# Gathering heads by DMA in every group instead of selector matmuls, in a two-layer transformer kernel

## The chip, the cores and the metric

The kernel runs on one core of a Trainium2 chip. The metric is the device time of one execution in microseconds (us). Engines are named as in the profile: PE is TensorE, PEld its weight loads, DVE is VectorE, ACT is ScalarE, POOL is GpSimd, and SP issues most DMAs.

## The reference, cut to what matters

```python
x = A_x                                              # 1 x 2048 x 1024, bfloat16
for layer in range(2):                               # written out twice in the reference
    q, k, v = split_heads(layernorm(x) @ wqkv)       # 32 heads of 32
    # each position attends to itself and 7 earlier ones, 2 apart
    idx    = pos[:, None] - 2 * arange(8)[None, :]
    logits = einsum("bhsd,bhswd->bhsw", q, k[idx]) * 32 ** -0.5   # -1e9 where idx < 0
    attn   = softmax(logits)
    x = x + merge(einsum("bhsw,bhswd->bhsd", attn, v[idx])) @ wo
    x = x + gelu(layernorm(x) @ w1 + b1) @ w2 + b2   # 3584 wide
```

## The kernel before

The work is done in eight groups (two layers times four blocks of 512 tokens). For a group `n`, PE computes QKV(n), WO(n), FFN1(n) and FFN2(n), one after the other without a gap. The attention itself is on DVE and is hidden under PE's matmuls of other groups. These are its parts (`P` is 128, `H` 32 heads, `NTT` 4 token tiles, `HP` 4, `W` 8 taps):

```python
def new_prod(n, c):            # q * k for the 8 taps of one chunk c, summed over chunks as a tree
    prod = bigp.tile([P, NTT, W, P], BF16, name="big")      # the pool "big" has 3 buffers
    vec.tensor_tensor(out=prod[:], in0=q..., in1=win_by_tile(k...), op=ALU.mult)
    ...                        # additions into the tree's open tiles

def head_sum(n, last=True):    # groups 0 and 1: the partitions of a head summed by selector matmuls
    for wh in range(2):
        for tb in range(NTT):
            mm(L[tb * H:(tb + 1) * H, wh * 4:(wh + 1) * 4, :], lhsT=smat[:], rhs=prod[:, tb, ...], ...)

def gather(n):                 # groups 2 to 7: moved by DMA, added on DVE
    Lq = bigp.tile([P, HP, W, P], BF16, name="big")
    for tb in range(NTT):
        pool.dma_start(Lq[tb * H:(tb + 1) * H, :, :, :], prod[:, tb, :, :])

def attend(n):                 # softmax over the 8 taps
    ...                        # e = the sum over a head, from Lq or from head_sum
    vec.tensor_reduce(out=mx[:], in_=L[:].rearrange("p w t -> p t w"), axis=AX.X, op=ALU.max)
    vec.tensor_tensor(out=e[:], in0=L[:], in1=mx..., op=ALU.subtract)
    act.activation(e[:], e[:], ACT.Exp, scale=SCALE)
    vec.tensor_reduce(out=z[:], in_=e[:].rearrange("p w t -> p t w"), axis=AX.X, op=ALU.add)
    vec.reciprocal(z[:], z[:])
    vec.tensor_tensor(out=a[:], in0=e[:], in1=z..., op=ALU.mult)

def spread(n):                 # the weights of a head to all its partitions, through DRAM
    for tb in range(NTT):
        pool.dma_start(a_d[:, :, tb * P:(tb + 1) * P], a[tb * H:(tb + 1) * H, :, :])
    for j in range(HP):
        pool.dma_start(abc[j::HP, :, :], a_d[:, :, :])

def av(n, c):                  # weights * v for one chunk: one product, three additions
    pv = bigp.tile([P, W, T], BF16, name="big")
    vec.tensor_tensor(out=pv[:], in0=s["abc"][:], in1=win(s["vT"][:, c, :]), op=ALU.mult)
    ...
    vec.tensor_tensor(out=s["oT"][:, c, :], in0=pv[:, 0, :], in1=pv[:, 1, :], op=ALU.add)
```

WO(n) contracts over the eight chunks of `oT`, so its first tile needs all eight. The order in which the parts are recorded, cut to the start:

```python
stage(q1, sides=at(6, attend, 0) + at(6, spread, 0) + at(6, hold) + each(new_prod, 1, 8, 1, 0, 4) + each(av, 0, 12, 1))
stage(q2, 18)                        # the first 18 of the 24 chunks of QKV(2)
new_prod(1, 4)
hold()
stage(gen_wo(0))
...
stage(gen_ffn1(0), sides=at(5, attend, 1) + at(5, spread, 1) + at(5, hold) + each(new_prod, 2, 2, 1)
      + at(10, gather, 2) + at(10, hold) + each(av, 1, 10, 2, 0, 4))
for n in range(1, N - 2):
    ...
    if n + 3 < N:
        stage(gen_ffn2(n), sides=at(0, attend, n + 2) + at(2, ln_a, n + 3))
```

`hold` makes every later DVE instruction stay behind what was recorded so far. Between holds a scheduler orders DVE's instructions.

## Time and profile before

| | before |
|---|---|
| time, median of 3 runs | 1232.97 us (1232.96 to 1233.32) |
| profiled span | 1231.1 us |
| PE busy | 1226.2 us, 5,789 matmuls |
| chain of waits | PE 99% |

The page's busy table of the kernel before:

```profile
PE 1226.2 (100%) x5789; PEld 632.7 (51%) x5789; DVE 870.0 (71%) x892; ACT 307.1 (25%) x491; POOL 123.0 (10%) x230
```

PE works all the time. Only fewer matmul columns, or a wait that goes away, could make the kernel faster, and there are hardly any waits. DVE is idle for 29% of the span on average, but an average says little about the stage where it is late. The timeline of PE shows where WO(0) and WO(1) stand. Its columns are start, duration, engine, source line, operation, output from input, shapes, count, and in brackets the idle time before with what ended it:

```profile
119.79 5.78 PE L118 MATMUL acc<-xnT,wt 128*128 128x512 bf16 x26
125.40 13.99 PE L118 MATMUL acc<-wt,oT 128*128 128x512 bf16 x64
139.23 20.88 PE L118 MATMUL acc<-xnT,wt 128*128 128x512 bf16 x96
...
246.94 13.98 PE L118 MATMUL acc<-wt,oT 128*128 128x512 bf16 x64
...
398.88 13.98 PE L118 MATMUL acc<-wt,oT 128*128 128x512 bf16 x64
```

The lines with `oT` are WO(0), WO(1) and WO(2). None has a wait in front, and each takes 13.98 to 13.99 us. The timeline of DVE tells how close that is. AV(0) begins and ends with these lines:

```profile
89.88 4.49 DVE L93 TENSOR_TENSOR big<-abc,vT 128x4096 bf16<-128x4096 bf16 x2
94.29 3.56 DVE L93 TENSOR_TENSOR big<-big 128x2048 bf16<-128x2048 bf16 x4
97.76 0.76 DVE L93 TENSOR_TENSOR oT<-big 128x512 bf16<-128x512 bf16 x2
98.43 4.49 DVE L93 TENSOR_TENSOR big<-abc,vT 128x4096 bf16<-128x4096 bf16 x2
...
123.41 0.76 DVE L93 TENSOR_TENSOR oT<-big 128x512 bf16<-128x512 bf16 x2
```

The eight chunks run in pairs (`x2`, `x4`): 8.55 us for two. The last `oT` is written at 124.2 us, 1.2 us before WO(0) starts.

### The profile page before, as it was taken

The page shows a single profiled execution, that of the slowest core. Times are in us where ns is not written, and L with a number is a line of the kernel's source. Part 1 is how long each engine was busy: PE and PEld are TensorE (multiplying, and loading weights), DVE is VectorE, ACT ScalarE, POOL GpSimd, SP SyncE. Part 2 cuts the span into 40 slices and gives each one's busy share as a digit, 9 for nine tenths or more (in the row PEclk, how much of TensorE's full clock was granted, in tenths as well). Part 3 has the DMA queues.
Part 4 walks back from the last instruction along what each step waited for, and adds up shares of the span by engine and source line. Part 5 has one row for each costly group of instructions (what it writes and reads, how often), then busy time and mean ns, then how long its engine had stood idle before and what let it go on. Part 6 is the DMA issues. An engine that isn't in the chain of part 4 may idle for free.

```text
span 1231.1 us, 13996 instructions
## 1 busy us (share of the span) xinstructions
PE 1226.2 (100%) x5789; PEld 632.7 (51%) x5789; DVE 870.0 (71%) x892; ACT 307.1 (25%) x491; POOL 123.0 (10%) x230
## 2 busy tenths in 40 slices
PE   9999999999999999999999999999999999999999
PEld 7666544456444564445544465444654444444444
DVE  8989899995996999376992779927599698012001
ACT  4343152014310143202431024310244101400310
POOL 3010011101021102200031000210000102000000
PEclk9999999999999999999999999999999999999999
DMA  9954677756487658756476565766666569546441
GB/s 301 289 179 142 177 220 183 210 140 230 147 197 226 177 165 180 220 170 186 149 187 222 172 171 169 174 222 196 171 183 157 186 200 198 166 158 196 153 136 53
DMA packets 219359, 226.63 MB, mean 184 GB/s; under 512 B 68562, under 2 KB 187488, under 8 KB 216224
## 3 DMA queue, kind: packets, MB, share of 16 engines
q1 hardware_dynamic: 214704, 208.69, 57.1%
q0 software_dynamic: 4592, 17.05, 5.7%
q8 instruction: 45, 0.74, 0.2%
q14 instruction: 18, 0.15, 0.0%
HBM read 197.40 MB, written 6.29 MB: 165 GB/s over the span
## 4 chain that ended last, share of the span: by engine, by line
PE 99%; DVE 0%; DMA 0%; ACT 0%; issue 0%
PE acc L118 99%; DMA x<-in_A_x_dram 0%; DVE stats L93 0%; PE acc L213 0%; PE L L118 0%; PE L L213 0%; ACT xnT L93 0%; DVE xn L93 0%; DVE x L93 0%; DVE mv L93 0%; PE acc L183 0%; DVE rstd L93 0%
## 5 line engine op out<-in xcount | busy, mean ns | idle before, releaser
L118 PE MATMUL acc<-xnT,wt 128*128 128x512 bf16 (+1 forms) x3392 | 720.8, 375 | 0.0
L118 PEld LDWEIGHTS <-wt 128*128 128x128 bf16 x3392 | 400.3, 119 | 318.8 <-issue 1.6
L118 PE MATMUL acc<-wt,hT 128*128 128x512 bf16 (+1 forms) x1820 | 388.1, 376 | 0.0
L118 PEld LDWEIGHTS <-hT 128*128 128x128 bf16 x1820 | 178.1, 98 | 209.0
L93 DVE TENSOR_TENSOR big<-big 128x2048 bf16<-128x2048 bf16 (+2 forms) x184 | 245.6, 1360 | 2.9
L93 ACT ACTIVATE hT<-acc,b1T 128x512 bf16<-128x512 f32 x224 | 152.5, 688 | 331.3 <-PE acc L118 331.2
L93 DVE TENSOR_TENSOR big<-qT,kT 128x4096 bf16<-128x4096 bf16 x64 | 143.8, 2286 | 26.7 <-ACT kT L93 26.1
L93 DVE TENSOR_TENSOR big<-abc,vT 128x4096 bf16<-128x4096 bf16 x64 | 144.8, 2287 | 24.3 <-DMA abc<-a_d 23.7
L93 DVE TENSOR_TENSOR tmp<-acc,b2bc 128x512 f32<-128x512 f32 x56 | 38.7, 690 | 148.4 <-PE acc L118 144.9
L93 ACT CAST qT<-acc 128x512 bf16<-128x512 f32 (+1 forms) x72 | 38.0, 542 | 341.4 <-PE acc L118 341.4
L118 PE MATMUL acc<-wt,oT 128*128 128x512 bf16 x448 | 97.9, 379 | 0.0
L93 DVE BATCH_NORM_STATS2 stats<-x 128x6 f32<-128x512 bf16 x128 | 83.5, 680 | 3.3 <-DMA x<-in_A_x_dram 2.6
L118 PEld LDWEIGHTS <-oT 128*128 128x128 bf16 x448 | 43.9, 98 | 52.8
L93 DVE TENSOR_TENSOR x<-acc,big 128x512 bf16<-128x512 f32 (+1 forms) x9 | 5.7, 633 | 90.0 <-PE acc L118 90.0
L93 POOL TENSOR_TENSOR rstd<-mv,eps_t 128x1 f32<-128x1 f32 x56 | 22.5, 402 | 434.4 <-DVE mv L93 434.3
L93 ACT CAST vT<-acc 128x512 bf16<-128x512 f32 x64 | 37.5, 586 | 83.1 <-PE acc L118 83.1
L93 ACT CAST kT<-acc 128x512 bf16<-128x512 f32 x64 | 37.3, 588 | 66.7 <-PE acc L118 66.6
L93 DVE TENSOR_TENSOR x<-acc,x 128x512 bf16<-128x512 f32 x64 | 42.6, 669 | 3.9 <-PE acc L118 3.8
L93 POOL TENSOR_TENSOR rstd<-rstd,mhalf 128x1 f32<-128x1 f32 x56 | 41.6, 743 | 4.4
L93 DVE TENSOR_SCALAR xn<-x,mv,rstd 128x1024 bf16<-128x1024 bf16 x52 | 28.4, 546 | 17.1 <-POOL rstd L93 16.9
L93 DVE TENSOR_TENSOR x<-tmp,x 128x512 bf16<-128x512 f32 x56 | 38.6, 690 | 1.6
L93 DVE TENSOR_REDUCE z<-e 128x128 f32<-128x1024 f32 x8 | 15.4, 1926 | 33.7 <-ACT e L93 33.7
(64 smaller groups left out, 252.0 us busy)
## 6 DMA issues: line engine op xcount, KB each, us to landing
wt<-in_B_w_dram SPq DMA_DIRECT2D x56, 1024.0 KB, 7.1
wt<-in_B_w_dram SPq DMA_DIRECT2D x64, 896.0 KB, 5.1
wt<-in_A_wqkv_dram SPq DMA_DIRECT2D x46, 1024.0 KB, 5.7
wt<-in_A_wo_dram SPq DMA_DIRECT2D x16, 1024.0 KB, 5.0
abc<-a_d POOLq DMA_DIRECT2D x32, 256.0 KB, 5.0
big<-big POOLq DMA_DIRECT2D x24, 256.0 KB, 7.0
x<-in_A_x_dram SPq DMA_DIRECT2D x16, 256.0 KB, 5.7
out_dram<-x SPq DMA_DIRECT2D x31, 128.0 KB, 2.4
```

Source lines behind the costliest of these rows:

```text
L93: inst = f(*args, **kwargs)
L118: return pe(nc.tensor.matmul(*args, **kwargs))
```

## The change: its intent, and the diff

The 16 selector matmuls leave PE; groups 0 and 1 get the gather by DMA that the other groups have. That puts three float32 additions per group on DVE. To pay for them, maximum and sum are folded by halves instead of reduced, the weights are spread from SBUF to SBUF without the trip through DRAM, and two products of group 2 move behind WO(1). The two accumulator banks of the selector matmuls join the pool `acc` (8 in place of 6). Cut to its core:

```diff
-        return psum.tile([P, T], F32, name="acc", bufs=6)
+        return psum.tile([P, T], F32, name="acc", bufs=8)
...
-    def head_sum(n, last=True):            # and all of its selector matmuls
...
     def gather(n):
-        for tb in range(NTT):
-            pool.dma_start(Lq[tb * H:(tb + 1) * H, :, :, :], prod[:, tb, :, :])
+        for j in range(HP):
+            pool.dma_start(Lq[:, j, :, :], prod[j::HP, :, :, :])
+
+    def fold(e, op):
+        t = iop.tile([P, W // 2, P], F32, name="tmp")
+        vec.tensor_tensor(out=t[:], in0=e[:, 0:4, :], in1=e[:, 4:8, :], op=op)
+        vec.tensor_tensor(out=t[:, 0:2, :], in0=t[:, 0:2, :], in1=t[:, 2:4, :], op=op)
+        vec.tensor_tensor(out=t[:, 0, :], in0=t[:, 0, :], in1=t[:, 1, :], op=op)
+        return t[:, 0, :]
...
     def spread(n):
-        for tb in range(NTT):
-            pool.dma_start(a_d[:, :, tb * P:(tb + 1) * P], a[tb * H:(tb + 1) * H, :, :])
         for j in range(HP):
-            pool.dma_start(abc[j::HP, :, :], a_d[:, :, :])
+            pool.dma_start(abc[j::HP, :, :, :], a[:])
...
-        stage(q1, sides=at(6, attend, 0) + at(6, spread, 0) + at(6, hold) + each(new_prod, 1, 8, 1, 0, 4) + each(av, 0, 12, 1))
+        stage(q1, sides=at(0, gather, 0) + each(new_prod, 1, 8, 1, 0, 2) + at(9, hold) + at(9, attend, 0) + at(9, spread, 0)
+              + at(10, new_prod, 1, 2) + at(10, hold) + each(av, 0, 12, 1))
         q2 = gen_qkv(2, defer=True)
         stage(q2, 18)
-        new_prod(1, 4)
+        hold()
+        new_prod(1, 3)
         hold()
         stage(gen_wo(0))
...       # in FFN1(0): products of group 2 only up to chunk 5; chunks 6 and 7, gather, attend and spread
...       # of group 2 go into the stage of QKV(3), behind WO(1); AV works by tiles of 128 tokens; in
...       # FFN2(n) a `hold` comes before the softmax
```

## The prediction

> **What bounds the kernel now.** TensorE. The page's busy table has PE at 1226.2 of 1231.1 us. The chain of waits gives it 99%; from 15.1 us to 1228.1 it is one run of matmuls. PE's waits sum to under 2 us. By the timeline 512-column matmuls follow each other every 0.216 us[...]. So only fewer PE columns can make it faster; a late DVE can make it slower.
>
> **What the change saves.** PE: 16 selector matmuls. They run four at a time: the chain of waits has two pieces of 0.55 us, 1.1 us in all. Perhaps 0.7 us more, as the early transposes get two accumulator banks instead of sharing one tile. The other savings are off PE: the folded maximum and sum should take 0.69 + 0.42 + 0.29 = 1.4 us[...] instead of 1.92 us; the spread loses its trip through DRAM (11 to 12.6 us from `a` to the first product where DVE waited for it). PE being full, they buy nothing.
>
> **What it costs.** DVE is the hidden limit until WO(1). By the timeline, the last product tree of AV(0) ends at 124.1 us and WO(0) starts at 125.4; that of AV(1) at 247.7, WO(1) starting at 246.9 and reaching that chunk 1.5 us later. Slack about 2 and under 1 us. In that stretch the change, by my count in the instruction order:
> - group 0: DVE has the products at 62.8, but the next ones need K of group 1 (copied at about 68.5). Two products and an add to 75.5, three float32 additions of gathered quarters (3.6 us, new), one product hoisted between them, mask, fold, subtract, exp (1.2 wait), fold, reciprocal: `a` at 89. Nothing stands between `a` and the first AV(0), so DVE now idles for the spread: four issues (2.1 us) and about 6 us landing. AV(0) runs 97.5 to 131.5 (8 x 4.28 us) instead of 89.9 to 124.1. WO(0) needs its last chunk at about 126: PE stalls about 5.5 us.
> - group 1: 3.6 us of additions come, 9.2 us (two group 2 products, two additions) move behind WO(1), where AV(2) was done 33 us early. DVE ends AV(1) at about 251.5, PE, shifted by the first stall, asks at about 252: 0 to 2 us of stall.
>
> Later groups keep 9 us or more of slack; faster spread and folds buy PE nothing there.
>
> **Sum.** 1233.0 - 1.1 - 0.5 + 5.5 + 0.2 = about 1237 us: 0.3% slower. Range 1232 to 1243. Faster by over 2%: 0.01; within: 0.96; slower: 0.03.
>
> **What would show it.** PE: 5,773 matmuls; a wait of WO(0)'s weight loads for DVE's `oT` of 4 to 7 us near 125 us, at most 2 us near 252. DVE waits for DMA `abc` about 8 us before the first AV(0) product. Group 0's `a` at about 89 us. `tensor_reduce` gone, folds near 1.4 us. AV adds with tile-wise strides keep 1.22, 0.69 and 0.42 us. From WO(2) on, PE time per group unchanged (151.9 us).
>
> **What would make it wrong.** A direct spread landing faster (4 us) shrinks the stall to about 3 us; one slowed by weight loads (the slowest gather took 12.3 us) doubles it. Strided AV adds being slower would cost on all eight chunks. Exp of group 1 stands behind 18 GELUs on ACT; if products are ready earlier than I count, that wait delays AV(1) and stalls WO(1) more.

The 224 matmuls of 512 columns of FFN2(0) started within 48.35 us in the kernel before (198.59 to 246.94 us, 0.216 us each), and the three steps of a fold took 0.69, 0.42 and 0.28 us in the kernel after. The first two sizes stand in the trace of the kernel before as well, with 0.69 and 0.42 us; the 0.29 us of the third had no trace behind it when it was written.

## The result, and the profile after

| | before | after |
|---|---|---|
| time, median | 1232.97 us (5 runs, 1232.82 to 1233.32) | 1245.75 us (5 runs, 1243.87 to 1246.14) |
| mean granted clock of a run | 1.0 | 0.996 to 0.997 |

The changed kernel gives a right result and is 1.0% slower: the ratio is 1.0100, with a 95% interval of 1.0085 to 1.0114. Ratios here are the mean time of one kernel's fast runs over that of the other's of the same rounds, so they are not quite the ratio of the medians quoted beside them.

The page's busy table of the kernel after:

```profile
PE 1227.3 (99%) x5773; PEld 632.6 (51%) x5773; DVE 868.6 (70%) x930; ACT 305.0 (25%) x491; POOL 92.9 (7%) x205
```

PE has 16 matmuls fewer and is busy longer than before; some matmuls must have got slower. The chain of waits, 99% PE before, is now 66% PE in a span of 1244.0 us, because it starts from a late DVE chain near WO(2). The timeline of PE after, at the same three places:

```profile
123.78 1.46 PE L117 MATMUL acc<-wt,oT 128*128 128x512 bf16 x6
126.80 0.39 PE L117 MATMUL acc<-wt,oT 128*128 128x512 bf16 x1 [1.56 <-DVE oT L92]
131.57 15.28 PE L117 MATMUL acc<-wt,oT 128*128 128x512 bf16 x57 [4.38 <-DVE oT L92]
...
253.74 1.46 PE L117 MATMUL acc<-wt,oT 128*128 128x512 bf16 x6
255.66 0.39 PE L117 MATMUL acc<-wt,oT 128*128 128x512 bf16 x1 [0.46 <-DVE oT L92]
257.98 12.48 PE L117 MATMUL acc<-wt,oT 128*128 128x512 bf16 x57 [1.93 <-DVE oT L92]
...
408.42 7.07 PE L117 MATMUL acc<-wt,oT 128*128 128x512 bf16 x32
416.51 1.89 PE L117 MATMUL acc<-wt,oT 128*128 128x512 bf16 x8 [1.02 <-DVE tmp L92]
418.92 1.89 PE L117 MATMUL acc<-wt,oT 128*128 128x512 bf16 x8 [0.52 <-DVE tmp L92]
422.32 3.61 PE L117 MATMUL acc<-wt,oT 128*128 128x512 bf16 x16 [1.51 <-DVE x L92]
```

All three products with WO now wait for DVE, and 57 matmuls of WO(0) take 15.28 us where 57 of WO(1) take 12.48. Cut by the starts of the stages in the two timelines, the 12.9 us of the two spans come from these places:

| stretch | before | after | difference |
|---|---|---|---|
| start to WO(0) | 125.40 | 123.78 | -1.62 |
| WO(0) | 13.83 | 22.91 | +9.08 |
| to WO(1) | 107.71 | 107.05 | -0.66 |
| WO(1) | 13.81 | 16.55 | +2.74 |
| to WO(2) | 138.13 | 138.13 | 0.00 |
| WO(2) | 13.82 | 17.35 | +3.53 |
| the rest | 818.4 | 818.2 | -0.2 |

**WO(0), the clock.** Windows of the kernel after around WO(0) (columns: from and to, length, then busy us and number of instructions of PE, PEld, DVE, ACT and POOL, the granted clock of PE, the DMA share and GB/s):

```profile
117.00:124.00 7.00, 7.00 (x35) 4.53 (x34) 6.83 (x6) 2.04 (x4) 0.00 (x0) 1.00 0.47 157
124.00:131.50 7.50, 1.62 (x7) 0.48 (x5) 7.26 (x8) 1.26 (x3) 0.00 (x0) 0.93 0.39 133
131.50:138.50 7.00, 6.93 (x20) 2.60 (x21) 6.90 (x5) 0.00 (x0) 0.00 (x0) 0.59 0.00 0
```

In the third window PE is busy but does 20 matmuls in 7.00 us, at a mean clock of 0.59; in the first it does 35. The trace's own clock record has one stretch at 0.5 while matmuls were still to do, 6.83 us long, from 130.46 to 137.29 us. The first 1.1 us of it still fall into the gap; half of the other 5.7 us is 2.9 us. So the gap of 4.38 us costs 4.38 us and then another 2.8 us (15.28 less 12.48) on the matmuls behind it. The clock fell 3.27 us after PE went idle (from 127.19 to 130.46 us); the last section has what the traces show of when it falls and comes back.

**WO(0), the gap.** The timeline of DVE after, for AV(0):

```profile
93.37 2.29 DVE L92 TENSOR_TENSOR big<-abc,vT 128x4096 bf16<-128x4096 bf16 x1 [5.29 <-DMA abc<-a]
95.70 1.96 DVE L92 TENSOR_TENSOR big<-big 128x2048 bf16<-128x2048 bf16 x2
97.69 0.43 DVE L92 TENSOR_TENSOR oT<-big 128x512 bf16<-128x512 bf16 x1
98.15 2.29 DVE L92 TENSOR_TENSOR big<-abc,vT 128x4096 bf16<-128x4096 bf16 x1
...
131.09 0.43 DVE L92 TENSOR_TENSOR oT<-big 128x512 bf16<-128x512 bf16 x1
```

AV(0) ends at 131.5 us, as predicted to the tenth, but through two errors that cancel. It starts at 93.37, not at 97.5: the spread landed sooner (5.29 us of waiting, not 8), and AV(0) goes chunk by chunk: from 93.37 to 98.15 is 4.78 us for one, against 8.55 us for two before. At that time two open product tiles of group 1 hold two of the three `big` buffers, so two chunks cannot be interleaved, and each operation waits for the one before it. The single file also makes the last gap as long as a chunk: the last `oT` comes 4.77 us after the one before, whenever the stage starts.

**WO(1)** waits 2.4 us for the last chunks of AV(1), which ended at 257.9 us, not at 251.5 as predicted. DVE had begun the rest of the work of group 1 later (the layer norm behind WO(0) ended at 152.8 us), and it waited 3.49 us for the gather of group 1.

**WO(2)** was predicted to be safe. Its waits are for `tmp` and `x`: WO(2) needs accumulator banks that FFN2(1) has filled, and DVE empties them late (such an emptying is called an eviction here). The timeline of DVE there:

```profile
401.14 0.69 DVE L92 TENSOR_TENSOR x<-tmp,x 128x512 bf16<-128x512 f32 x1
409.09 4.49 DVE L92 TENSOR_TENSOR big<-abc,vT 128x4096 bf16<-128x4096 bf16 x2 [7.26 <-DMA abc<-a]
413.50 2.35 DVE L92 TENSOR_TENSOR big<-big 128x2048 bf16<-128x2048 bf16 x2
415.77 0.68 DVE L92 TENSOR_TENSOR tmp<-acc,b2bc 128x512 f32<-128x512 f32 x1
```

After an eviction at 401.14 us DVE stands idle for 7.26 us before a product of AV(3), whose weights are still under way, and only then come the last evictions of FFN2(1), from 415.77 us on. DVE took its instructions in order: none of the evictions behind the product ran in those 7.26 us. In the kernel before, the first product of AV(3) started at 400.45 us, just behind the last of those evictions. Now the scheduler puts two products ahead of them, and the program has no `hold` at this place. The weights are late too: `a` of group 3 is ready at 395.9 us in place of 381.9, because AV(2), which moved behind WO(1), ended later and that softmax comes after it (its first addition starts at 378.6 us in place of 365.7). The chain of waits shows the spread of group 3 taking 11.00 us from its last issue here, while the queue of the weight loads takes 86.5% of the DMA engines between 395 and 412 us. From the first issue to the last landing it is 12.7 us, against about 12.4 us through DRAM in the kernel before: at this place the direct spread is no faster.

### The profile page after: what moved, and what is told of

Read it like the earlier page. It is cut to its first block, busy times and chain, and to the rows that moved or that the text cites. A ratio compares the mean times of both kernels' runs of the same rounds, so it can differ in the third digit from the quotient of the medians.

```text
span 1244.0 us, 13986 instructions
## 1 busy us (share of the span) xinstructions
PE 1227.3 (99%) x5773; PEld 632.6 (51%) x5773; DVE 868.6 (70%) x930; ACT 305.0 (25%) x491; POOL 92.9 (7%) x205
## 4 chain that ended last, share of the span: by engine, by line
PE 66%; DVE 1%; DMA 1%; POOL 0%; issue 0%; DVEq 0%; POOLq 0%
PE acc L117 66%; DMA abc<-a 1%; DVE big L92 1%; DVE x L92 0%; DVE tmp L92 0%; POOL abc L92 0%; POOL rstd L92 0%; DVE a L92 0%; DVE xn L92 0%; DVE z L92 0%; DVE mv L92 0%; DVEq L92 0%; POOLq L92 0%
## 5 line engine op out<-in xcount | busy, mean ns | idle before, releaser
L92 DVE TENSOR_TENSOR big<-big 128x1024 bf16<-128x1024 bf16 (+2 forms) x184 | 246.7, 1359 | 2.6
L117 PE MATMUL acc<-wt,oT 128*128 128x512 bf16 x448 | 101.8, 387 | 11.4 <-DVE oT L92 8.3
L92 POOL TENSOR_TENSOR rstd<-mv,eps_t 128x1 f32<-128x1 f32 x56 | 16.4, 293 | 543.4 <-DVE mv L92 543.4
L92 POOL TENSOR_TENSOR rstd<-rstd,mhalf 128x1 f32<-128x1 f32 x56 | 30.9, 551 | 4.4
```

Source lines behind the costliest of these rows:

```text
L92: inst = f(*args, **kwargs)
L117: return pe(nc.tensor.matmul(*args, **kwargs))
```

## The experiments

Each edit is relative to the kernel after unless another is named. "Before" means runs of the kernel before in the same rounds.

### Evictions first

```diff
             stage(gen_ffn2(n), sides=at(0, hold) + at(0, attend, n + 2) + at(2, ln_a, n + 3))
+            hold()
```

> The changed kernel with one more ordering point behind FFN2 of group 1 and later ones, so that no AV product of the next group can stand ahead of the last evictions of FFN2 on DVE. Theory (an AV product that waits for its spread blocks the evictions whose banks WO(2) needs): WO(2) on PE goes from 17.35 us back to 13.8, nothing else moves, about 1242.2 us. Rival (WO(2) is late because the DVE is late by its whole backlog since WO(0)): the wait stays or moves to other instructions of WO(2) or WO(3), 1245 to 1246 us.

Measured: 1241.69 us (1241.09 to 1243.89), ratio 1.0071 [1.0056, 1.0086]. WO(2) takes its normal time without a wait (timeline of PE):

```profile
407.27 13.98 PE L117 MATMUL acc<-wt,oT 128*128 128x512 bf16 x64
```

The 3.5 us lost there are the order of DVE's instructions, not the amount of work. The medians differ by 4.1 us; in this profile WO(1) also waits 1.27 us instead of 2.4, because DVE waited 1.47 us for the gather of group 1 instead of 3.49, which the edit does not touch.

### PE kept busy through the gap

Matmuls on a constant are put before the last two chunks of WO(0)'s first tile, so that PE waits as long but without idling.

```diff
                 for c in range(NCH):
+                    if n == 0 and tt == 0 and dh == 0 and c >= 6:
+                        for _ in range(6 if c == 6 else 18):
+                            mm(junk[:], lhsT=ident[:], rhs=ident[:].unsqueeze(1).to_broadcast([P, NTT, P]), start=True, stop=True)
                     mm(ps[:], lhsT=oT[:, c, tt * P:(tt + 1) * P], rhs=..., start=(c == 0), stop=(c == NCH - 1))
```

> The changed kernel with 24 matmuls on a constant (6 and 18, about 5.2 us in all) put into the two waits of WO(0), results unused. Theory[...]: granted clock stays 1.0, the 57 matmuls after the gap take 12.5 instead of 15.3 us, time 2.8 us shorter, about 1243 us, although PE has more work. Rival (those matmuls are slow because of weight loads or accumulator banks): they still take 15 us, time 1245.5 us or more.

The theory put the slow matmuls down to the idle gap, 4.38 us in the kernel after, and to the 6.83 us at a clock of 0.5 that followed.

Measured: 1241.13 us (1240.2 to 1242.19), ratio 1.0061 [1.0044, 1.0078]; the clock is 1.0 throughout. The timeline of PE, and the window that had 0.59:

```profile
127.10 4.05 PE L117 MATMUL acc<-ident 128*128 128x512 bf16 x18
131.64 12.48 PE L117 MATMUL acc<-wt,oT 128*128 128x512 bf16 x57 [0.50 <-DVE oT L92]
...
131.50:138.50 7.00, 6.86 (x32) 3.15 (x33) 6.90 (x5) 0.00 (x0) 0.00 (x0) 1.00 0.00 0
```

WO(0) gets through its chunk at the same time (131.64 against 131.57) and the 57 matmuls behind take 12.48 us. So 2.8 us were the clock, caused by the idling. The whole gain was 4.6 us, more than expected: the waits at WO(1) and WO(2) shrank too (to 1.23 and 1.51 us), while a new one of 1.83 us for `xnT` came at the start of FFN1(0), which PE now reached earlier. The smaller waits are not DVE's work: the layer norm behind WO(0) ended at 152.8 us as before, and the gather of group 1 was issued at 171.2 us in both profiles. It landed after at most 6.2 us here and 8.1 there, and DVE waited 1.62 us for it instead of 3.49.

### The third product in the softmax's gap

A second `hold` makes the product (1, 2) run behind the softmax of group 0, while the spread is under way.

```diff
               + at(9, hold) + at(9, attend, 0) + at(9, spread, 0)
-              + at(10, new_prod, 1, 2) + at(10, hold) + each(av, 0, 12, 1))
+              + at(9, hold) + at(10, new_prod, 1, 2) + at(10, hold) + each(av, 0, 12, 1))
```

> The changed kernel with the third group 1 product forced behind the softmax of group 0, where the DVE waits for the spread, not between its additions. Expected: a of group 0 is done 2.2 us earlier (85.8 us), AV(0) ends near 129.3 instead of 131.5, WO(0)'s waits fall from 5.9 to 3.7 us. If the longer of them (about 2.2 us) is too short to drop the clock, the half clock stretch goes as well and the time is 1240.6; if the clock drops all the same, 1243.4 us. AV(0) still runs one chunk at a time (4.77 us each). Rival (the softmax time before AV(0) doesn't set WO(0)'s wait): 1245.5 us.

Measured: 1243.45 us (1242.89 to 1244.24), ratio 1.0083 [1.0068, 1.0098]. AV(0) starts 1.3 us earlier (92.07) and the first of the two waits is gone, but the gap of 4.38 us is not. It is the cadence of the single file: 4.77 us from one `oT` to the next, less the 0.39 us of a matmul. The half clock lasted 3.41 us this time.

### Two buffers for AV(0)

The product (1, 2) moves behind AV(0), so that two `big` buffers are free in it.

```diff
-              + at(10, new_prod, 1, 2) + at(10, hold) + each(av, 0, 12, 1))
+              + at(10, hold) + each(av, 0, 12, 1))
...
         hold()
+        new_prod(1, 2)
         new_prod(1, 3)
```

> The changed kernel with the third group 1 product moved behind AV(0). Theory (two open group 1 product tiles leave AV(0) one of three product buffers, so its chunks run singly at 4.77 us instead of in pairs at 4.28): AV(0) runs in pairs, takes 34.2 instead of 38.2 us, starts 2.2 us earlier and ends near 125.3; WO(0) waits under 1 us, no half clock; WO(1)'s and WO(2)'s delays stay at 2 to 4 us each: about 1237 us. Rival (the single file is due to the order of waits, not to buffers): 4.77 us per chunk stay, AV(0) ends near 129.3, 1241 to 1243.5 us.

Measured: 1241.11 us (1239.15 to 1242.48), ratio 1.0059 [1.0043, 1.0074]. The timeline of DVE, then that of PE:

```profile
92.97 4.49 DVE L92 TENSOR_TENSOR big<-abc,vT 128x4096 bf16<-128x4096 bf16 x2 [5.24 <-DMA abc<-a]
...
126.51 0.75 DVE L92 TENSOR_TENSOR oT<-big 128x512 bf16<-128x512 bf16 x2
```

```profile
126.98 12.81 PE L117 MATMUL acc<-wt,oT 128*128 128x512 bf16 x57 [0.46 <-DVE oT L92]
...
154.08 6.22 PE L117 MATMUL acc<-xnT,wt 128*128 128x512 bf16 x16 [3.92 <-DMA xnT<-xn]
```

AV(0) runs in pairs and ends at 127.3 us in place of 131.5, from nearly the same start (the 2.2 us that it was to start earlier came to 0.4); WO(0)'s wait falls to 0.46 us. That is the buffers. But the expected 1237 us are missed: the product that was moved now stands before the layer norm that follows WO(0), and FFN1(0) waits 3.92 us for it, which again halves the clock for 6.83 us. A delay removed at one deadline of DVE reappeared at the next.

### Group 2's two products not moved

Products (2, 6) and (2, 7) and the gather of group 2 go back before WO(1).

> The changed kernel with the two group 2 products (and their additions and the gather of group 2) back in front of WO(1), where the kernel before has them. Theory (DVE work bounds the stretch up to WO(1)): 9.2 us more DVE work there adds about 9 us to WO(1)'s wait, which is over 4 us long and so also halves the clock: 1255 to 1258 us. Rival (the move itself is what hurts WO(2)): WO(2)'s 3.5 us go and WO(1) changes little, 1242 to 1245 us.

A halved clock behind a wait of over 4 us had been seen at the gap of 4.38 us in the kernel after.

```diff
+ each(new_prod, 2, 6, 1, 4, 6)                      ->  each(new_prod, 2, 6, 1, 4, 8)
+ at(8, hold) + each(av, 1, 10, 2, 0, 5)             ->  at(10, gather, 2) + at(10, hold) + each(av, 1, 10, 2, 0, 5)
each(new_prod, 2, 0, 1, 6, 8) + at(1, gather, 2)     ->  (left out in QKV(3))
```

Measured: 1253.23 us (1252.48 to 1253.53), ratio 1.0161 [1.0148, 1.0175]. WO(1) waits 7.69 and 3.95 us instead of 2.4 in all, and the clock is at 0.5 for 13.65 us, most of it during these waits. WO(2)'s waits are gone, which is why the time stays under the 1255 expected. But the order is not better there, as the timeline of DVE shows:

```profile
405.25 4.49 DVE L92 TENSOR_TENSOR big<-abc,vT 128x4096 bf16<-128x4096 bf16 x2 [1.66 <-DMA abc<-a]
...
415.38 0.69 DVE L92 TENSOR_TENSOR tmp<-acc,b2bc 128x512 f32<-128x512 f32 x1 [3.37 <-PE acc L117]
```

The same two products of AV(3) stand ahead of the last four evictions; PE comes to WO(2) 11.3 us later (at 419.71 us), so this time DVE is done first and waits for PE. In these runs the order cost time only where the weights came later than PE needed its banks. This part of the change is needed: without it the loss at WO(1) would be 9.2 us of waiting larger.

### The selectors kept, with the other parts of the change

The kernel before, with the folds and a direct spread from SBUF to SBUF (four DMAs, in the partition order of before).

```diff
-        for tb in range(NTT):
-            pool.dma_start(a_d[:, :, tb * P:(tb + 1) * P], a[tb * H:(tb + 1) * H, :, :])
-        for j in range(HP):
-            pool.dma_start(abc[j::HP, :, :], a_d[:, :, :])
+        for tb in range(NTT):
+            src = a[tb * H:(tb + 1) * H, :, :]
+            src = bass.AP(tensor=src.tensor, offset=src.offset, ap=[list(src.ap[0]), [0, HP], [1, W * P]])
+            pool.dma_start(abc[:, tb, :, :], src)
```

> The kernel before with only the two other parts of the change: folded softmax and the direct spread from SBUF to SBUF (its old partition order, hence four transfers that repeat each partition four times), selector matmuls and the old order of products kept. Theory (the loss at WO(0) and WO(1) comes from gathering groups 0 and 1, fold and spread are off PE's path): WO(0) and WO(1) start without a wait over 1 us, 1233 us within 0.7; if the faster spread by itself lets an AV product slip ahead of evictions, a wait of 1 to 4 us shows at WO(2) only, up to 1236.5 us. Rival (direct spread or fold harms): waits at WO(0), 1238 us or more.

Measured: 1253.41 us (1252.14 to 1253.62), ratio 1.0161 [1.0146, 1.0176]. WO(0) and WO(1) have no wait, as the theory said; the size was missed by far. The timeline of PE shows one long gap, in the middle of FFN2(1) (four more, in FFN2(2), (3) and (5), sum to 2.7 us), and that of DVE its cause:

```profile
392.23 24.23 PE L117 MATMUL acc<-wt,hT 128*128 128x512 bf16 x98 [13.83 <-DVE tmp L92]
```

```profile
385.95 4.49 DVE L92 TENSOR_TENSOR big<-abc,vT 128x4096 bf16<-128x4096 bf16 x2 [11.68 <-DMA abc<-a]
...
391.50 0.68 DVE L92 TENSOR_TENSOR tmp<-acc,b2bc 128x512 f32<-128x512 f32 x1
```

This is the fault of WO(2) again, larger: two products of AV(3), which wait 11.68 us for their weights, stand ahead of all eight evictions of FFN2(1), not only of the last four. Whether it also matters that there are 6 accumulator banks instead of 8 was not tested. The clock is at 0.5 for 17.07 us, of which 11.1 fall into the wait itself; on the matmuls behind, 3 us are lost by it. The changed spread, which was to buy nothing, is what moved the products up; the next two runs separate it from the folds.

### The same, evictions first

The kernel of the run before, with the `hold()` of the first experiment.

> The kernel before with fold and direct spread (the one that took 1253.4 us) and the ordering point behind FFN2 of groups 1 and later. Theory (all of its 20 us come from an AV(3) product that stands ahead of the evictions of FFN2(1), waits for its spread, and lets PE idle and its clock drop): 1233 us within 0.7. Rival (the direct spread slows weight loads): 1236 us or more.

Measured: 1235.6 us (1235.4 to 1235.76), ratio 1.0018 [1.0005, 1.0031]. The gap of 13.83 us is gone, and 17.8 us with it. Of the 2.2 us that are left over the kernel before, 1.5 are two waits of 1.07 and 0.47 us for `tmp` in FFN2(5), the branch of the loop to which no `hold` was added. So the place of AV's products against the evictions explains nearly all that this kernel lost.

### The folds alone

The kernel before with `fold` in place of the reductions and nothing else.

> The kernel before with the folded softmax alone; the order of instructions shows that AV(3) then stays behind the evictions of FFN2(1). Theory: 1233 us within 0.5, though the folds take 0.5 us less than the reductions in each group: DVE time that is off PE's path buys nothing. Rival (shorter softmax helps PE): 1230 us or less.

Measured: 1233.33 us (1233.16 to 1233.6), ratio 0.9999 [0.9985, 1.0013]. The folds are shorter (0.69 and 0.75 us against a reduction of 1.92 us) and buy nothing, because PE does not wait for them. One product of AV(3) stands ahead of the last eviction of FFN2(1) here too, at 399.88 us, but its weights are there and it costs nothing.

### The remedies together

The evictions first, AV(0) in explicit pairs, the softmax of group 0 ahead of the products of group 1, two products in the gap of the spread, the other two behind AV(0), and the statistics of a later layer norm in the gap of the gather.

```diff
+    def av2(n, c):             # two chunks, their operations interleaved in program order
+        ...
-        stage(q1, sides=at(0, gather, 0) + each(new_prod, 1, 8, 1, 0, 2) + at(9, hold) + ... + each(av, 0, 12, 1))
+        stage(q1, sides=at(0, gather, 0) + at(0, hold) + at(0, ln_stats_ahead, 3) + at(0, hold) + at(10, attend, 0) + at(10, spread, 0)
+              + at(10, hold) + each(new_prod, 1, 10, 0, 0, 2) + at(10, hold)
+              + [(12 + c, lambda c=c: av2(0, c)) for c in range(0, NCH, 2)])
...
+        new_prod(1, 2)
         new_prod(1, 3)
```

> The changed kernel with all remedies: statistics of group 3 put into the DVE gap before the gather lands (they leave the stretch before WO(1)), softmax of group 0 before the group 1 products, two of these products as filler for the spread, AV(0) in pairs, evictions of FFN2 ahead of AV. Theory: no PE wait over 0.5 us at WO(0), WO(1), WO(2); what is left is the gain of 1.1 us for the selectors and about 0.5 us at the start: 1231.4 us, 0.1% faster than the kernel before. Rival (a part of the loss is inherent in gathering groups 0 and 1): waits of 2 us or more remain at WO(1), 1234 us or more.

Measured: 1235.87 us (1235.47 to 1236.04), ratio 1.0021 [1.0009, 1.0034]. All waits at WO(0), WO(1) and WO(2) are gone. One is left, in the timeline of PE at the start of FFN1(0):

```profile
151.81 50.19 PE L117 MATMUL acc<-xnT,wt 128*128 128x512 bf16 x224 [3.17 <-DMA xnT<-xn]
```

The layer norm behind WO(0) is late by the product that stands before it, and the clock is at 0.5 for 3.41 us after that (from 153.12 us).

### The layer norm first

As the last, with product (1, 3) behind the layer norm.

```diff
         new_prod(1, 2)
-        new_prod(1, 3)
         hold()
...
-        stage(q2, sides=each(new_prod, 1, 0, 1, 4, 8))
+        stage(q2, sides=at(0, new_prod, 1, 3) + each(new_prod, 1, 0, 1, 4, 8))
```

> The combined version with one of the two group 1 products that stood between AV(0) and the layer norm of WO(0) moved behind that layer norm, with the two additions. Theory (in the combined version the 3.2 us wait of FFN1(0) for its transposes and the half clock after it come from the layer norm being 5 us late): no wait there, clock 1.0 throughout, 1231 to 1231.8 us, some 0.1 to 0.15% faster than the kernel before. Rival (the transposes are late by themselves, behind weight loads): the wait stays, 1235.5 us; or the moved work comes back as a wait of 2 us or more at WO(1), 1234 us.

Measured: 1235.39 us, but from 1233.3 to 1239.19 in six runs, ratio 1.0019 [1.0007, 1.003]. The three slowest of the six have a mean clock of 0.997 to 0.998, the others 1.0. The wait for `xnT` is gone; a new one has come (timeline of PE, then of ACT):

```profile
165.68 34.69 PE L117 MATMUL acc<-xnT,wt 128*128 128x512 bf16 x160 [2.34 <-ACT hT L92]
```

```profile
163.64 1.28 ACT L92 ACT_TABLE_LOAD   x1 [13.18 <-DVE big L92]
```

`hT`, the output of the GELU, is allocated in memory that `q` and `k` of group 1 had before. ACT may not write it until DVE has done the last product of group 1; in the kernel before it waited 4.01 us for that, here 13.18. The accumulator banks fill up in the meantime; PE's 2.34 us are a wait for ACT to empty one. A product moved behind one deadline ran into the next.

### One product less (wrong result)

The last kernel with one product of group 1 left out: one multiplication, and one addition into the tree.

```diff
     def new_prod(n, c):
+        if (n, c) == (1, 5):
+            b = s["prods"].pop()
+            vec.tensor_tensor(out=s["prods"][-1][:], in0=s["prods"][-1][:], in1=b[:], op=ALU.add)
+            return
```

> The kernel of the run before (layer norm first) with one window product of group 1[...] left out, so its result is wrong on purpose. Theory: what is left over in that run is VectorE work before the last product of group 1, which the GELU output waits for. Then the load of the GELU table starts near 159 us in place of 163.6, TensorE does not wait for hT in FFN1(0), the clock is 1.0 in every run and the time falls from 1235.4 to 1231-1232. Rival: the remaining 2.4 us over the kernel before have another cause, in a later group; then the time stays at 1234-1236 us although the wait for hT is gone.

Cut is a duration that the traces do not bear out: in the kernel after one multiplication takes 2.28 us and one addition 2.29, 4.57 us for both.

Measured: 1231.02 us (1230.77 to 1231.61), ratio 0.9982 [0.9968, 0.9995], with a wrong result as intended. The table load starts at 158.58 us, PE waits for nothing from WO(0) on, and the clock is 1.0 in all five runs. So what the run before this still lost was work of DVE before deadlines in the first two groups. The time is 2.1 us under the kernel before; the saving that the prediction promised on PE, 1.1 to 1.6 us, fits into that.

### Layer norm on ScalarE

The kernel with the layer norm first, with a right result again: the four normalisations behind WO(0) go to ScalarE, which is idle there. GpSimd computes one more small number for each.

```diff
-        xn = ln_norm(t, mv, rstd)
+        if on_act:                         # in WO(0) only; else ln_norm as before
+            pool.tensor_scalar(out=nb[:], in0=mv[:, 0:1], scalar1=rstd[:], scalar2=-1.0, op0=ALU.mult, op1=ALU.mult)
+            xn = lnp.tile([P, D], BF16, name="xn", bufs=3)
+            act.activation(xn[:], x[t][:], ACT.Identity, bias=nb[:], scale=rstd[:])
```

> The kernel of the run with the layer norm first, with the four normalisations of group 0's second layer norm moved from VectorE to ScalarE (which waits for the matmuls in most of that stretch), so that VectorE has 2.2 us less work and up to four waits for rstd (2.1 us together) fewer before the last product of group 1. The result must stay right. Theory (the GELU output waits for VectorE's products): the load of the GELU table starts at 160 to 161.5 us in place of 163.6, TensorE's wait for hT in FFN1(0) is under 0.3 us, the clock is 1.0 in every run, and the time is 1231 to 1231.8 us, 0.1 to 0.2% under the kernel before. If ScalarE's normalisations come so late that the transposes of layer norm do, TensorE waits for xnT at the start of FFN1(0) instead, and the time stays at 1233 us or above.

Measured: 1238.74 us (1237.75 to 1239.83), ratio 1.0044 [1.003, 1.0057]. On DVE it did what was expected (the table load starts at 160.49 us and PE does not wait for `hT`), yet PE waits 5.22 us for `xnT`, since the fourth normalisation came at 149.23 us. The timeline of GpSimd, for the last two of the four:

```profile
136.84 0.19 POOL L92 TENSOR_TENSOR rstd<-mv,eps_t 128x1 f32<-128x1 f32 x1 [2.41 <-DVE mv L92]
137.11 0.55 POOL L92 TENSOR_TENSOR rstd<-rstd,mhalf 128x1 f32<-128x1 f32 x1
137.76 0.26 POOL L92 TENSOR_SCALAR nb<-mv,rstd 128x1 f32<-128x1 f32 x1
140.29 2.05 POOL L92 TENSOR_TENSOR rstd<-mv,eps_t 128x1 f32<-128x1 f32 x1 [2.27 <-DVE mv L92]
142.42 2.61 POOL L92 TENSOR_TENSOR rstd<-rstd,mhalf 128x1 f32<-128x1 f32 x1
145.13 4.07 POOL L92 TENSOR_SCALAR nb<-mv,rstd 128x1 f32<-128x1 f32 x1
```

The same three operations, on one element per partition, took 1.0 us and then 8.7. At 140.06 us DVE had started its large products, which in the kernels so far it could not, since it waited for `rstd` itself. In the trace the slow ones stand beside such products; that these are the cause is a theory here, and the next run tests it.

### The table ahead, the last normalisation on VectorE

Three normalisations on ScalarE, the fourth on DVE, so that DVE waits for GpSimd and starts no product beside it; and a dummy GELU that loads the table before it is needed.

```diff
-        if on_act:
+        if split and tt < NTT - 1:         # the fourth tile by ln_norm on VectorE, as before
             ...                            # the three lines of the run before
     def gen_ffn1(n):
+        if n == 0:
+            early_table = lnp.tile([P, 1], F32, name="nb")
+            act.activation(early_table[:], eps_t[:], ACT.Gelu_apprx_tanh)
+            act.hold()
```

> The kernel of the run with the layer norm first, with two changes, and a right result. Three of the four normalisations of group 0's second layer norm go to ScalarE; the fourth stays on VectorE, so that VectorE waits for GpSimd's small operations and starts no large product beside them. A dummy GELU of one element per partition loads the GELU table before WO(0) ends. Theory (VectorE's work before the last product of group 1 holds up the GELU output, and the 1.28 us of the table load stand behind it): the last product's end falls by about 2 us to about 161.5 us, the first GELU output starts there instead of at 164.9, TensorE waits less than 0.3 us in FFN1(0), and the time is 1231 to 1232 us. If GpSimd's operations in the run before took 8.7 us for another reason than VectorE's products beside them, the fourth normalisation is late again and TensorE waits for xnT at 148.7 us, with 1236 us or more.

Measured: 1231.82 us (1231.33 to 1232.57, six runs) beside 1233.21 for the kernel before, ratio 0.9987 [0.9975, 1.0], with a right result. The timelines of GpSimd and PE:

```profile
140.49 0.19 POOL L92 TENSOR_TENSOR rstd<-mv,eps_t 128x1 f32<-128x1 f32 x1 [2.27 <-DVE mv L92]
140.76 0.55 POOL L92 TENSOR_TENSOR rstd<-rstd,mhalf 128x1 f32<-128x1 f32 x1
```

```profile
163.04 34.69 PE L117 MATMUL acc<-xnT,wt 128*128 128x512 bf16 x160 [0.29 <-ACT hT L92]
```

GpSimd's two operations take 0.19 and 0.55 us again when DVE runs no product beside them. PE's only wait from WO(0) on is 0.29 us, and the clock is 1.0 in all six runs. With the same selectors gone, 13.9 us lie between this kernel and the one after (medians of different rounds), all of it in the order and the place of work off PE. Against the kernel before it is 0.1% at most, and the interval reaches 1.0; it is not a gain to count on.

## Why the prediction was wrong

The prediction had the direction and the mechanism of the first stall, and put the whole at 1237 us with an upper end of 1243; the measured 1245.75 lie outside.

Right, by the traces:
- PE bounds the kernel, and the selectors save 0.55 us each time; 5,773 matmuls are left.
- `a` of group 0 is ready at 88.1 us (predicted 89). The folds take 1.5 us (predicted 1.4). The trace has 0.69 us for the operation on 512 float32 elements, and 0.75 for the two small ones together.
- AV's operations kept their durations with tile-wise strides: 2.29, 1.22, 0.69 and 0.42 us before, 2.29, 1.22, 0.69 and 0.41 after (means).
- The wait for `oT` near 125 us is 5.9 us in all (predicted 4 to 7), near 252 us 2.4 (predicted at most 2).
- From the end of WO(2) on nothing changed: the rest of the span differs by 0.2 us.

Wrong, by the step:
- **"PE stalls about 5.5 us"** was taken as the whole price of WO(0), which was 9.1. The wait was 5.9 us; the term left out is the clock, 2.8 us, which the prediction did not think of (0.3 us are left unexplained). The run with PE kept busy took exactly it away. That the stall came out right was luck: "AV(0) runs 97.5 to 131.5 (8 x 4.28 us)" had the spread too slow (8 us of wait against 5.29) and AV(0) too fast (4.28 us a chunk against 4.77). The third open tile in a pool of three buffers had been counted as work and not as a buffer; in the run with two buffers AV(0) ended 4.3 us earlier (127.3 against 131.5).
- **"0 to 2 us of stall" at WO(1)** measured 2.7 us in the stage. DVE ended AV(1) 6.4 us later than counted: it inherited the late layer norm of WO(0), and the wait of 3.49 us for its gather was not in the count. That wait is not fixed: it was 1.62 us in the run with PE kept busy, where the gather started at the same time.
- **"Later groups keep 9 us or more of slack; faster spread and folds buy PE nothing there"** cost 3.5 us at WO(2). The slack of AV was real, but AV was not what PE waited for. With the changed spread the scheduler put AV's products ahead of evictions that PE needs, and DVE waited in order (7.26 us). The run with evictions first, and the pair with the selectors kept (1253.4 and 1235.6 us), show it; and since the folds alone change nothing (1233.3), it is the spread, with the tile-wise AV that came with it, and not the folds alone. Why the scheduler then orders so was not looked into: on the chip the spread was no faster there (12.7 us against about 12.4). The order hurt because the weights were late as well; `a` of group 3 came 14 us later than in the kernel before, and where PE itself came 11.3 us later (the products not moved) the same order cost nothing. The order of DVE's instructions could have been read before the run.
- The savings at the start were nearly as predicted: 1.62 us to WO(0), of which 0.55 are selectors and 0.66 a wait of the early transposes; the rest, 0.4 us, is within the variation of the start: in the profiles of the kernel after and of five runs whose PE work is the same up to there, WO(0) starts between 123.8 and 125.1 us.

In sum: predicted +4.0, measured +12.8 (medians). The parts that were mis-sized are WO(0) by 3.6, WO(1) by 2.5 (2.7 against the 0.2 in the sum) and WO(2) by 3.5, less 0.9 us by which the other stretches saved more than counted. What stays open is small: why WO(1) and WO(2) change by 1 to 2 us in runs that do not edit them. By the traces the landing of the gather of group 1 is a part of it; no run separates it from the rest.

## What to carry to other kernels

When one engine is full and another feeds it just in time, moving work to the second can be paid at every deadline that it has (here 9.1, 2.7 and 3.5 us at WO(0), WO(1) and WO(2)), so list all of them first (operands, freed accumulator banks, memory that waits to be reused, transposes for the next stage) and not only the next one. An idle gap on PE can cost more than its length (gaps of 3.17 us and more did here, those of up to 2.34 us did not in the profiled runs), and a pool with one buffer too few can cost per item rather than once (here 4.77 us a chunk in place of 4.28). After a DMA has been changed, read the order of the instructions again, because an engine that takes them in order may now stand waiting for it in front of work that was urgent, as DVE did here for 7.26 us, and for 11.68 us with the selectors kept.

## What the traces show of the hardware

- The clock of PE. In the traces of the kernels before and after the clock changes only at whole steps of 3.413 us from the start of its record: the stretches up to the fall at the end are 1225.385 us (359 steps) in the one, and 126.293, 6.827 and 1105.918 us (37, 2 and 324 steps) in the other. Cut into such windows, the kernel after has 3.28 us of idle PE in the window that ended in the fall at WO(0), 2.22 us in the one that ended in the fall at the kernel's end, and at most 1.56 us in every other window at full clock. After the fall at WO(0), full clock did not come back behind the window with 1.11 us of idling, but behind the next, which had none. In the remedies together the fall at 153.12 us came behind 2.10 us of idling in the 3.413 us before it. So a gap of 3.17 us can be enough (the remedies together). The same gap of 4.38 us gave 6.83 us at half clock in the kernel after and 3.41 us with the third product in the softmax's gap; that this comes from where it lay in the windows is the author's reading. Of that slow stretch only the part behind the gap cost time in the kernel after, about half of it: 5.7 us at half clock cost the 57 matmuls 2.8 us.
- DMA. The spread's four DMAs of 256 KB took 2.8 us in the median near 90 us, where the queue of the weight loads took 27.2% of the DMA engines (86 to 96 us), but 10.2 us at WO(2), where it took 86.5% (395 to 412 us).
- VectorE. The four dependent operations of a chunk took 4.77 us, and the same interleaved with those of a second chunk 4.28 us a chunk.
- ScalarE. The 17 table loads of the kernel after took 1.283 us each in the mean, and behind 15 of them the next instruction started 1.29 us after the start of the load (behind the other two it waited for its operand, and started after 1.85 and 7.65 us).
- GpSimd beside VectorE. Small GpSimd operations of 0.19, 0.55 and 0.26 us became 2.05, 2.61 and 4.07 us beside VectorE's products in the run with the layer norm on ScalarE: 7.7 us more for the chain of three. Where VectorE ran no product beside them, in the run with the table ahead, the first two took 0.19 and 0.55 us.
